# An attention and feed-forward kernel: one scale for each unit of the first weight, sums of weight blocks moved, products of a block scheme reordered, elu written with a rectifier

## The chip, the cores and the metric

The kernel runs on one core of a Trainium2 chip. The metric is the device time in microseconds (us) of one execution. The engines are named as in the profile: TensorE (PE, its weight loads PEld), VectorE (DVE), ScalarE (ACT), GpSimd (POOL) and SyncE (SP), which issues nearly all DMA transfers. Each engine works off its own instructions in order.

## The reference, cut to what matters

```python
# q, k, v: (8, 12, 448, 64) float32; w_in: (768, 2048), w_out: (2048, 768), both float64
scores = q @ k^T / sqrt(64) - log(448)
attn   = sigmoid(scores) @ v
x      = attn.transpose(0, 2, 1, 3).reshape(3584, 768)
h      = x @ w_in
g      = where(h > 0, h, exp(min(h, 0)) - 1)        # elu
out    = g @ w_out                                  # (3584, 768) float32
```

## The kernel before, in words

All products run on TensorE in float16. Each operand is held as two float16 parts: the value times a power of two, rounded (high part, ScalarE), and what is left of it (low part, VectorE). A product is three: high·high, high·low, low·high. The scales are powers of two taken from sums of magnitudes: a matmul with ones (or one with a diagonal, L188, whose result is `pb`) gives them to all partitions, and VectorE takes the exponent.

**Attention.** Twelve heads are six head pairs `hp` per batch. A pair's queries and keys are loaded (`raw`), measured (`measure_next`: maxima on VectorE), scaled (`scale_next`) and split (`split_next`: high parts L606, low parts L609, a transposing DMA L614 from `nat` to `qk`, the split values, and then `load_pair`, which issues the eight loads of a later pair on SP's queue). The main loop (from L1481) runs over batches 2 to 7 and their pairs: scores (L643), sigmoid (ScalarE L667), split of the sigmoid (L687, L688), products with the values (L701). Between these, `fill` puts in matmuls of the second layer of the batch before (L1102).

**First layer.** `w_in` is prepared in the first stage in eight units of 256 columns. Its tokens stand in a hand-written string, `ORDER`, run from left to right; the order on each engine is the order in the program. Per unit: `l` load, `A` `b` `B` `d` bit operations that make float32 of float64, `C` the sum of magnitudes on TensorE, `D` the scale on VectorE, `E` the high part on ScalarE (L323), `F` the low part on VectorE. `C` of two units writes one PSUM tile, and `D`, after the second `C`, makes one scale for both (`swi`, L308); so `E` of the first unit waits for the second unit. Batches 0 and 1 use these parts directly, in the first stage. In the same string `X0` to `X95` are second-layer steps of batch 0, `K` is one step of the sums told next, `W` a store of plain weight blocks.

**Block scheme.** From batch 2 on the first layer is done with seven products of blocks instead of eight (the scheme of Strassen and Winograd), for each of four column groups `w` of two units. The weight enters as seven blocks: three plain ones and four sums and differences. They lie in a DRAM tensor, `blend`, and 168 loads of 384 KB (a ring of ten) bring them back to the space of `wi`. The plain ones are stored by DMA straight from `wi` (`store_parts`). The sums are made once, by the generator `sums_of_parts` (L344): per unit VectorE adds high and low part (L357) and forms the sums; then each of the four is split again, high part on ScalarE (L363), low part on VectorE (L366), into one of three rooms of the tile `room`, which SP's queue stores (L373). A room is used again by the piece three further on, whose high part waits until that store has landed. `make_sums(n)` does n steps, of which a unit has eight: 29 tokens `K` beside the second layer of batch 0, sixteen calls beside the first layer of batch 1 (`beside_first`), and the rest in batch 2's attention, five per pair in pairs 0 to 2 and what remains in pair 3, after which the ring's first ten loads are issued.

The products of a batch run in the order `USES` (L936), each of 18 matmuls (L993) into a PSUM bank: products 1, 4, 6 and 7 into X (which `w` shares), 2 into A, 3 into B, 5 into Y. `behind(k, w)` is what follows product k on the other engines: copies that hand a partial sum on (X to A, L1063 X to B, Y to `s5`), adds of `s5` (L1042, into `c`), and elu. Elu is three operations:

```python
nc.scalar.activation(e, src, AF.Exp, scale=m)                                  # L1007
nc.vector.tensor_scalar(e, e, 1.0, -1.0, op0=ALU.min, op1=ALU.add)             # L1011
nc.vector.scalar_tensor_tensor(e, src, m, e, op0=ALU.mult, op1=ALU.max)        # L1012
```

Half of a column group is done as one tile of 896 columns (`e2`), the other as two of 448 (`e1`). `parts_of_g` splits the result into `g` (L1026, L1031). `order_of_blocks` says after which of the 28 products a part of the next pairs' preparation is put in.

## Time and profile before

| | |
|---|---|
| runs | 1209.97, 1215.53, 1210.32 us; median 1210.32 |
| profiled execution | 1208.79 us, span 1207.0 us |
| mean granted TensorE clock | 0.986 |
| TensorE busy | 1128.0 us, 93% of the span (weight loads 719.1, beside it) |
| VectorE busy | 865.7 us, 72% |
| ScalarE busy | 706.8 us, 59% |
| GpSimd busy | 65.3 us, 5% |
| DMA | 164.65 MB, mean 136 GB/s |

The span is the part of the profiled execution between its first and last instruction. Busy times of different engines overlap; a share is a mean over stages. The stages stand in the trace, from the span's start, at: the preparation of `w_in` and the attention of batches 0 and 1 up to 125 us, first and second layer of batch 0 to 247, first layer of batch 1 to 309, then for each of batches 2 to 7 attention (beside the second layer of the batch before) and block stage: 309 to 414.6 and 414.6 to 470.2 for batch 2.

### The profile page before, as it was taken

What the parts mean: (1) busy time and instruction counts of PE and PEld (TensorE: products, weight loads), DVE (VectorE), ACT (ScalarE), POOL (GpSimd) and SP (SyncE); (2) the same over time, 40 slices, a digit from 0 to 9 for tenths busy, and PEclk for the clock granted to TensorE, in tenths of its full rate; (3) what the DMA queues carried; (4) which work ended last, traced back from release to release, by engine and by line L of the source; (5) the groups of instructions that cost most, each with busy time, mean ns of one, the idle gap of its engine ahead of it and who ended that gap; (6) DMA issues with size and microseconds to landing.
All of it is one profiled execution on the core that took longest, in us unless ns stands there. A gap on an engine that the chain in (4) does not pass through costs nothing.

```text
span 1207.0 us, 22288 instructions
## 1 busy us (share of the span) xinstructions
PE 1128.0 (93%) x8626; PEld 719.1 (60%) x8626; DVE 865.7 (72%) x1783; ACT 706.8 (59%) x996; POOL 65.3 (5%) x276
## 2 busy tenths in 40 slices
PE   6788998889889999999899999999899999999998
PEld 2332454445445597559855697559855597559965
DVE  2777788777878577887777577887777577877600
ACT  5778765434656446684666556685566556685500
POOL 0000000100001000100001000100001000100000
PEclk9899999989999999999999999999999999999999
DMA  9883533444146376445834177445835167425200
GB/s 237 204 233 91 183 108 112 157 149 96 40 109 178 103 227 210 97 91 179 246 93 98 48 212 226 97 90 154 261 94 103 52 200 237 97 45 169 75 27 27
DMA packets 234714, 164.65 MB, mean 136 GB/s; under 512 B 170096, under 2 KB 209008, under 8 KB 234608
## 3 DMA queue, kind: packets, MB, share of 16 engines
q1 hardware_dynamic: 234608, 163.23, 49.1%
q8 instruction: 67, 1.10, 0.4%
q14 instruction: 39, 0.32, 0.1%
HBM read 124.65 MB, written 22.02 MB: 122 GB/s over the span
## 4 chain that ended last, share of the span: by engine, by line
PE 58%; DVE 20%; ACT 9%; DMA 6%; issue 4%; SPq 2%; POOL 1%; DVEq 0%; ACTq 0%; POOLq 0%
PE po L1102 22%; PE psc L643 7%; PE pav L701 6%; PE X L993 6%; PE po_r L1102 5%; PE ph L894 4%; DVE g L1031 2%; PE A L993 2%; PE Y L993 2%; ACT sg L667 2%; DMA vn<-in_v_dram 1%; PE pav L719 1%; DVE ea L1012 1%; PE B L993 1%; DVE nat L609 1%
## 5 line engine op out<-in xcount | busy, mean ns | idle before, releaser
L1102 PE MATMUL po<-wo,g 128*128 128x384 f16 x2304 | 391.6, 328 | 7.0 <-DVE wo L466 4.5
L1102 PEld LDWEIGHTS <-g 128*128 128x128 f16 x2688 | 258.9, 98 | 211.0 <-issue 46.7
L993 PEld LDWEIGHTS <-wi 128*128 128x128 f16 x3024 | 288.6, 98 | 25.1 <-issue 23.7
L688 DVE SCALAR_TENSOR_TENSOR at<-sg,at 128x896 f16<-128x896 f32 x126 | 132.5, 1087 | 62.3 <-ACT at L687 62.0
L993 PE MATMUL X<-wi 128*128 128x224 f16 x1296 | 133.0, 259 | 9.1 <-DVE c L1042 6.6
L667 ACT ACTIVATE sg<-psc,bias,sc 128x896 f32<-128x896 f32 x108 | 114.3, 1090 | 35.6 <-PE psc L643 35.4
L643 PE MATMUL psc<-qk 64*128 64x448 f16 (+2 forms) x960 | 109.8, 379 | 8.3 <-ACT qk L1286 3.7
L606 ACT ACTIVATE nat<-raw,sc 128x384 f16<-128x384 f32 (+1 forms) x108 | 52.8, 536 | 109.7 <-POOL sc L577 103.6
L894 PE MATMUL ph<-xh,wi 128*128 128x448 f16 x576 | 114.0, 359 | 0.0
L687 ACT ACTIVATE at<-sg 128x896 f16<-128x896 f32 x126 | 113.4, 945 | 0.6
L894 PEld LDWEIGHTS <-wi 128*128 128x128 f16 x576 | 56.8, 99 | 59.2 <-issue 9.0
L609 DVE SCALAR_TENSOR_TENSOR nat<-raw,sc,nat 128x384 f16<-128x384 f32 (+1 forms) x108 | 52.5, 526 | 28.3 <-ACT nat L606 27.7
L701 PE MATMUL pav<-at,vn 128*64 128x448 f16 x648 | 69.0, 358 | 0.0
L1102 PE MATMUL po_r<-wo,g 128*128 128x384 f16 x384 | 67.1, 335 | 0.0
L1007 ACT ACTIVATE eb<-c,msc 128x896 f32<-128x896 f32 x24 | 25.0, 1042 | 66.5 <-DVE c L1042 66.5
L643 PEld LDWEIGHTS <-qk 64*128 64x128 f16 (+1 forms) x864 | 30.3, 97 | 52.9 <-issue 32.7
L1112 DVE TENSOR_SCALAR o<-po,osc 128x384 f32<-128x384 f32 x48 | 29.3, 611 | 41.6 <-PE po L1102 38.6
L993 PE MATMUL X<-xh,wi 128*128 128x224 f16 x432 | 45.4, 259 | 9.6 <-DVE ea L1012 9.6
L701 PEld LDWEIGHTS <-vn 128*64 128x64 f16 x648 | 33.9, 110 | 33.0 <-issue 14.2
L1031 DVE SCALAR_TENSOR_TENSOR g<-ea,msc,g 128x448 f16<-128x448 f32 x48 | 32.5, 678 | 17.8 <-ACT g L1026 17.8
L993 PE MATMUL Y<-xh,wi 128*128 128x224 f16 x432 | 45.3, 259 | 0.0
L993 PE MATMUL A<-xh,wi 128*128 128x224 f16 x432 | 45.3, 259 | 0.0
(166 smaller groups left out, 1409.3 us busy)
## 6 DMA issues: line engine op xcount, KB each, us to landing
wi<-blend SPq DMA_DIRECT2D x168, 384.0 KB, 4.6
stage<-in_moe_w_in_dram SPq DMA_DIRECT2D x16, 768.0 KB, 7.1
wo<-in_moe_w_out_dram SPq DMA_DIRECT2D x13, 768.0 KB, 4.5
raw<-in_q_dram SPq DMA_DIRECT2D x96, 96.0 KB, 3.3
raw<-in_k_dram SPq DMA_DIRECT2D x96, 96.0 KB, 2.9
out_dram<-o SPq DMA_DIRECT2D x48, 192.0 KB, 1.9
rv<-in_v_dram SPq DMA_DIRECT2D x36, 192.0 KB, 2.7
blend<-room SPq DMA_DIRECT2D x32, 192.0 KB, 1.9
```

The lines of the kernel that those rows point to most:

```text
L606: nc.scalar.mul(hi, src, s)
L609: nc.vector.scalar_tensor_tensor(lo, src, s, hi, op0=ALU.mult, op1=ALU.subtract)
L643: nc.tensor.matmul(psc[:, j, :S] if g < NC else psc[rows[x], j, :S], kk[rows[j], o], qq[rows[j], :S], start=(n == 0), stop=(n == n_parts - 1),
L667: a = nc.scalar.activation(sg, psc[:, :, :S], AF.Sigmoid, bias=bias, scale=scale)
L687: nc.scalar.mul(parts[0], sg, 2.0**ATOP)
L688: nc.vector.scalar_tensor_tensor(parts[1], sg, 2.0**ATOP, parts[0], op0=ALU.mult, op1=ALU.subtract)
L701: nc.tensor.matmul(pav[rows[j], :S], vv[i][:, j * NC + g if g < NC else 2 * NC + j], sg[k][:, j], start=(g == 0 and n == 0), stop=False,)
L894: nc.tensor.matmul(ph[:, :S], wi[:, NU - 1 - f // WF, f % WF * NK + c, wj], hidden_of(b, c)[:, xj], start=(n == 0), stop=(n == 3 * NK - 1),)
L993: nc.tensor.matmul(to[:, j * HS : (j + 1) * HS], block[:, j, c, wj], rhs(k, c, xj), start=(k in (1, 5) and j == 0 and n == 0), stop=(j == ...
L1031: nc.vector.scalar_tensor_tensor(rows_of_g(w, 1, odd, lo, hi), x, gs, rows_of_g(w, 0, odd, lo, hi), op0=ALU.mult, op1=ALU.subtract,)
L1102: nc.tensor.matmul(po[:, :HM], lh(gj, f), wo[:, i, f, wj], start=(n == 0), stop=(n == 3 * NF - 1),)
L1112: nc.vector.tensor_scalar(o, po[:, :HM], sc, None, op0=ALU.mult)
```

## The change

- Each weight unit gets its own scale (`D` after each `C`); that of a pair's second unit is at least that of its first. Where two units are used together, from batch 2 on, the second unit's scale `wq` holds, and `wt`, the ratio of a unit's own scale to it, is multiplied into sums and plain blocks. `wi` is laid out with rows of 256 columns and one load per unit.
- Plain blocks are no longer stored from `wi`: ScalarE copies their two parts, scaled, into the three rooms (two instructions each). A unit now has seven steps, each with one or no store. 19 tokens `K` are left beside the second layer, none after `X86`; beside batch 1's first layer a step stands only at the eleven turns without other work.
- In batch 2's attention the steps stand behind `scale_next` (two) and behind `split_next` and `measure_next` (three; in pair 3 all the rest, then the ring's loads). `measure_next` of pair 0 is called earlier.
- The products of the block stage are reordered, with the places of the copies, of the splits and of the preparation.
- Elu in the block stage: exp and rectifier on ScalarE, the second in place in PSUM (or `c`), then one instruction on VectorE, min(e - 1, relu). All of `e1` is split at once.

```diff
-V1.1 C0 b1 l2 V1.2 v12 V1.3 A1 M1 v4 T2 v5 H1 n1 H0 T3 I1 Y2 Q1 q5 I0 Y3 S2.0 S2.1 G2.0
-N1 G2.1 S2.2 B1 V2.0 G2.2 q4 S3.3 d0 b2 S3.0 V2.1 G3.3 M2 l3 V2.2 C1 S3.1 k5 D1 G3.0 E0
...
-X50 K h10 X51 p10 X52 h11 X53 p11 X54 h12 X55 p12 X56 h13 X57 h14 p13 p14 X58 K h15 X59
-h16 p15 p16 X60 h17 X61 h18 p17 p18 X62 K W0 X63 X64 K O3 X65 K X66 W1 X67 K X68 K X69
-X70 K W2 X71 K X72 X73 K X74 K W3 X75 X76 K X77 K X78 W4 X79 K X80 K O4 X81 X82 K W5 X83
-K X84 X85 K X86 K W6 X87 X88 K X89 K X90 W7 X91 K X92 K X93 X94 K X95 K O5
+V1.1 C0 b1 l2 V1.2 D0 v12 V1.3 A1 M1 v4 T2 v5 H1 n1 H0 T3 I1 Y2 Q1 q5 I0 Y3 S2.0 S2.1
+G2.0 N1 G2.1 S2.2 B1 V2.0 G2.2 q4 S3.3 d0 b2 S3.0 V2.1 G3.3 M2 l3 V2.2 E0 S3.1 k5 C1
...
+X58 K h15 X59 h16 p15 p16 X60 h17 X61 h18 p17 p18 X62 K X63 X64 K O3 X65 X66 K X67 X68 K
+X69 X70 K X71 X72 K X73 X74 K X75 X76 K X77 X78 K X79 X80 K O4 X81 X82 K X83 X84 K X85
+X86 K X87 X88 X89 X90 X91 X92 X93 X94 X95 O5
...
+            queue.dma_start(st.bitcast(U64), src[:, :, u * WF * P : (u + 1) * WF * P])
...
         def scale():
+            least = [wp[:, f.start - 1 : f.start]] if u % 2 else []
+            sum_magnitude(wp[:, f], st["sums"][:, : WF * P], *least)
...
+        nc.gpsimd.tensor_tensor(wt, wp, wr, op=ALU.mult)
...
     def sums_of_parts():
...
+        def high(x):
+            t = next_out()
+            nc.scalar.mul(t[1][:, 0], block(full, x), r)
+            return t
+
+        def low(x, t):
+            nc.vector.scalar_tensor_tensor(
+                t[1][:, 1], block(full, x), r, t[1][:, 0], op0=ALU.mult, op1=ALU.subtract
+            )
+            store(t, {"22": 3, "21": 1, "11": 0, "12": 2}[x])
...
+        def copy(x, slot):
+            t = next_out()
+            for h in range(2):
+                nc.scalar.mul(t[1][:, h], block(wi[:, NU - 1 - u, h], x), r)
+            store(t, slot)
 
         for u in range(NU):
+            r = wt[:, u * WF : u * WF + 1]
+            parts = wi[:, NU - 1 - u]
+            for i in range(2):
+                c = slice(i * HK, (i + 1) * HK)
+                nc.vector.tensor_tensor(full[:, c], parts[:, 0, c], parts[:, 1, c], op=ALU.add)
+                copy("11" if i else "12", 4 + (not i))
+                yield
             add("22", "21", "22", ALU.add)
             add("21", "11", "21", ALU.subtract)
+            copy("22", 6)
             yield
             add("11", "22", "11", ALU.subtract)
             add("12", "12", "11", ALU.subtract)
+            one = high("22")
             yield
+            two = high("21")
+            low("22", one)
             yield
+            one = high("11")
+            low("21", two)
             yield
+            two = high("12")
+            low("11", one)
             yield
+            low("12", two)
...
     USES = [(1, 0), (5, 0)]
-    for w in range(NW):
...
-        USES += [(6, w), (2, w), *ahead[0], (7, w), (3, w), *ahead[1], (4, w)]
+    for w in range(NW - 1):
+        late = [(6, w + 1), (4, w)] if w == NW - 2 else [(4, w), (6, w + 1)]
+        USES += [(6, 0)] * (not w) + [(2, w), (5, w + 1), (7, w), (1, w + 1), (3, w), *late]
+    USES += [(k, NW - 1) for k in (2, 7, 3, 4)]
...
         def exps(e, src, w):
-            a = nc.scalar.activation(e, src, AF.Exp, scale=m[:, 0, 4 * w : 4 * w + 1])
+            scale = m[:, 0, 4 * w : 4 * w + 1]
+            nc.scalar.activation(e, src, AF.Exp, scale=scale)
+            a = nc.scalar.activation(src, src, AF.Relu, scale=scale)
...
-        def rests(e, src, w):
-            nc.vector.tensor_scalar(e, e, 1.0, -1.0, op0=ALU.min, op1=ALU.add)
-            nc.vector.scalar_tensor_tensor(
-                e, src, m[:, 0, 4 * w : 4 * w + 1], e, op0=ALU.mult, op1=ALU.max
-            )
+        def rests(e, src):
+            nc.vector.scalar_tensor_tensor(e, e, -1.0, src, op0=ALU.add, op1=ALU.min)
...
     def beside_first(f):
-        for step in order.get(f, []):
+        for step in order.get(f, [make_sums]):
             step()
-        make_sums()
...
                 for t in range(2):
                     p.halves(t)
-                if b == 2 and hp <= HK:
-                    make_sums()
+                if hp == 0:
+                    measure_next()
...
                 p.scores(2)
                 p.sigmoid(2)
-                if hp == 0:
-                    measure_next()
...
                 p.halves(2)
                 if hp % 2:
                     first.halves(NC)
-                if b == 2 and hp <= HK:
-                    make_sums()
...
                     scale_next()
                     pb_tag = "pav1"
+                    if b == 2:
+                        make_sums(2)
...
                     done[1].finish()
-                if b == 2 and hp <= HK:
-                    make_sums()
-                if b == 2 and hp == HK:
-                    make_sums(8 * NF)
-                    for i in range(RING):
-                        load_block(i)
...
                     split_next()
-                    if b == 2 and hp < HK:
-                        make_sums(2)
                     measure_next()
+                    if b == 2:
+                        make_sums(3 if hp < HK else 8 * NF)
+                    if b == 2 and hp == HK:
+                        for i in range(RING):
+                            load_block(i)
```

## Rows read from the trace of the kernel before

**Rows 1.** Busy time by stretch: start:end, length, busy us per engine, granted clock, DMA.

```profile
0.00:125.00 125.00, 97.94 (x511) 37.05 (x511) 80.49 (x160) 92.12 (x91) 1.81 (x15) 0.96 0.76 188
...
247.00:309.00 62.00, 57.49 (x292) 28.87 (x290) 47.56 (x115) 27.37 (x59) 4.68 (x15) 0.94 0.34 97
309.00:414.60 105.60, 94.29 (x663) 49.13 (x661) 78.31 (x163) 61.91 (x86) 7.80 (x26) 0.94 0.42 117
414.60:470.20 55.60, 51.92 (x528) 50.03 (x524) 41.31 (x90) 28.41 (x47) 3.70 (x17) 1.00 0.69 204
...
1088.80:1139.90 51.10, 51.10 (x526) 49.95 (x523) 35.06 (x68) 25.89 (x42) 0.61 (x2) 1.00 0.47 144
```

The columns are PE, PEld, DVE, ACT and POOL, each with its count of instructions, then the granted clock, the DMA share and GB/s.

**Rows 2.** Waits: engine and line, waited for, us in total, times, longest us.

```profile
ACT wi L323 <- DVE swi L308: 8.4, 4, 3.0
...
PE pav L701 <- ACT sg L667: 6.5, 3, 2.5
...
PE psc L643 <- ACT qk L1286: 3.7, 2, 3.5
```

**Rows 3.** TensorE in time, 240 to 420: start, us, instruction, idle before it.

```profile
255.08 0.17 PE L188 MATMUL pb<-dg,ones 128*128 128x4 bf16 x1 [4.51 <-DVE dg L182]
...
317.75 0.74 PE L643 MATMUL psc<-qk 64*128 64x448 f16 x6 [1.51 <-ACT sg L667]
...
325.05 0.17 PE L188 MATMUL pb<-dg,ones 128*128 128x12 bf16 x1 [3.04 <-DVE dg L182]
...
357.95 0.17 PE L188 MATMUL pb<-dg,ones 128*128 128x12 bf16 x1 [4.39 <-DVE room L366]
...
397.20 2.12 PE L643 MATMUL psc<-qk 64*128 64x448 f16 x12 [2.27 <-DMA qk<-nat]
```

**Rows 4.** All engines in order of time, 344 to 360.

```profile
347.13 1.55 SPq L614 DMA_TRANSPOSE qk<-nat  x1
...
349.30 0.74 PE L643 MATMUL psc<-qk 64*128 64x448 f16 x6
...
351.39 0.23 DVE L182 TENSOR_SCALAR dg<-blocks,trm 128x12 bf16<-128x12 bf16 x1
...
354.50 3.80 SPq L373 DMA_DIRECT2D blend<-room  x4
356.85 0.51 ACT L363 CAST room<-room 128x384 f16<-128x384 f32 x1 [5.76 <-DMA blend<-room]
...
357.80 1.09 ACT L667 ACTIVATE sg<-psc,bias,sc 128x896 f32<-128x896 f32 x1
```

**Rows 5.** The tile `room` from 200 to 420: instructions, ns min/median/max.

```profile
L357 DVE TENSOR_TENSOR room<-room x32: 540/558/559, 208.3 to 369.6; 128x384 f32<-128x384 f32 x32
L363 ACT CAST room<-room x32: 494/510/513, 213.9 to 378.1; 128x384 f16<-128x384 f32 x32
...
DMA to landing us min/median/max: 1.8/1.9/4.4
```

**Rows 6.** TensorE in time, 414.6 to 470.4: its waits in batch 2's block stage.

```profile
437.50 1.89 PE L993 MATMUL X<-xh,wi 128*128 128x224 f16 x18 [0.83 <-DVE ea L1012]
...
450.83 1.89 PE L993 MATMUL X<-xh,wi 128*128 128x224 f16 x18 [1.09 <-DVE ea L1012]
...
463.56 1.89 PE L993 MATMUL X<-wi 128*128 128x224 f16 x18 [0.49 <-ACT B L1063]
...
468.45 1.89 PE L993 MATMUL X<-wi 128*128 128x224 f16 x18 [1.27 <-DVE c L1042]
```

**Rows 7.** Groups by line and form: busy us, mean ns; idle before, releasers.

```profile
L1007 ACT ACTIVATE eb<-c,msc 128x896 f32<-128x896 f32 x24 | 25.0, 1042 | 66.5 <-DVE c L1042 66.5
L1011 DVE TENSOR_SCALAR ea<-ea 128x448 f32<-128x448 f32 x48 | 18.6, 388 | 5.4 <-ACT ea L1007 5.4
...
L1007 ACT ACTIVATE ea<-A,msc 128x448 f32<-128x448 f32 x24 | 15.0, 624 | 23.8 <-DVE msc L876 23.4
...
L1061 ACT ACT_TABLE_LOAD x6 | 7.7, 1283 | 0.1
```

More of the change, by code (lines that the diff above doesn't have):

```diff
@@ L250, in signed, with sum_magnitude @@
         )
-    def sum_magnitude(dst, sums):
+    def sum_magnitude(dst, sums, *least):
         m = sb.tile([P, 1], F32, tag="alw", name="alw", bufs=2)
         nc.vector.tensor_reduce(m, sums, axis=AX.X, op=ALU.max)
-        nc.vector.tensor_scalar(m, m, TINY, None, op0=ALU.max)
+        more = {"op1": ALU.max} if least else {}
+        nc.vector.tensor_scalar(m, m, TINY, *(least or [None]), op0=ALU.max, **more)
         nc.vector.tensor_scalar(
@@ L291, in sums @@
         def sums():
[L292 to L308 removed]
+            st["sums"] = ps.tile([P, 512], F32, tag="pm", name=f"si{u}", bufs=PB)
+            add_sums(st["sums"][:, : WF * P], st["t"], True, True, ones_in)
+        def scale():
+            least = [wp[:, f.start - 1 : f.start]] if u % 2 else []
+            sum_magnitude(wp[:, f], st["sums"][:, : WF * P], *least)
+            s = st["s"] = sb.tile([P, 1], F32, tag="sw", name=f"swi{u}", bufs=2)
+            nc.vector.reciprocal(s, wp[:, f][:, 0:1])
         def lower():
             nc.vector.scalar_tensor_tensor(
[L312 removed]
+                d[:, 1], st["t"], st["s"], d[:, 0], op0=ALU.mult, op1=ALU.subtract
             )
@@ L343, in sums_of_parts @@
+        nc.gpsimd.tensor_tensor(wt, wp, wr, op=ALU.mult)
     def sums_of_parts():
-        names = "11", "12", "21", "22"
         n = HK * P
         room = sb.tile([P, 7, 2 * n], F16, tag="xh", name="room")
-        one = {x: room[:, i].bitcast(F32) for i, x in enumerate(names)}
-        slots = {"22": 3, "21": 1, "11": 0, "12": 2}
-        def whole_of(u, i):
-            x = room[:, 2 * i : 2 * i + 2].bitcast(F32).rearrange("p b (c x) -> p (b c) x", x=P)
-            hi, lo = (wi[:, NU - 1 - u, i * NK : (i + 1) * NK, h] for h in range(2))
-            nc.vector.tensor_tensor(x, hi, lo, op=ALU.add)
@@ L356, in add @@
-        def add(x, y, z, op):
-            nc.vector.tensor_tensor(one[x], one[y], one[z], op=op)
-        def parts(i):
-            return room[:, 4 + i % 3].rearrange("p (c h x) -> p h c x", c=HK, h=2)
-        def high(x, i):
-            nc.scalar.copy(parts(i)[:, 0], one[x].rearrange("p (c x) -> p c x", c=HK))
-        def low(x, i):
-            nc.vector.tensor_tensor(
-                parts(i)[:, 1], one[x].rearrange("p (c x) -> p c x", c=HK), parts(i)[:, 0],
-                op=ALU.subtract,
-            )
@@ L371, in store, with block, next_out @@
-        def store(u, x, i):
+        full = room[:, :4].rearrange("p b x -> p (b x)").bitcast(F32)
+        full = full.rearrange("p (c x) -> p c x", c=NK)
+        def block(t, x):
+            c, f = HK * (x[1] == "2"), P * (x[0] == "2")
+            return t[:, c : c + HK, f : f + P]
+        def add(x, y, z, op):
+            nc.vector.tensor_tensor(block(full, x), block(full, y), block(full, z), op=op)
+        out = 0
+        def next_out():
+            nonlocal out
+            out += 1
+            t = room[:, 4 + out % 3]
+            return t, t.rearrange("p (c h x) -> p h c x", c=HK, h=2)
@@ L372, in store @@
+        def high(x):
[5 more added lines that the diff above has]
+                t[1][:, 1], block(full, x), r, t[1][:, 0], op0=ALU.mult, op1=ALU.subtract
+            )
+            store(t, {"22": 3, "21": 1, "11": 0, "12": 2}[x])
+        def store(t, slot):
             w, j = divmod(u, 2)
[L373 to L375 removed]
```

216 lines of the change are left out of this document (87 added, 129 removed).

## The prediction, made before the changed kernel had run

> **What bounds the kernel now.** I read four views in this order. First the table of busy time by stretch. Of the six block stages (the first layer of batches 2 to 7) the first is 55.6 us long with 3.7 us of TensorE idle, the next four are within 0.3 us of it, and the sixth, 51.1 us, has no idle time [rows 1]. So from 414.6 us on there is little more to win than those 3.7 us a batch, while whatever delays TensorE is paid in full. The other idle time stands before 414.6 us: 27 us in the first 125, 4.5 in 247 to 309, 11.3 in 309 to 414.6, and there the granted clock is below 1 as well. A mean of 0.94 means 12% of the stretch at the lower level: 7.4 us of 62.0 and 12.7 us of 105.6, of which half is lost, 3.7 and 6.3 us [rows 1]. Then the waits and TensorE's own gaps, which say what ended the idle time: in the first stage ScalarE, which had itself waited four times (8.4 us) for the weight scale of step D [rows 2]; later the sums of the weight blocks [rows 3, 4]; in the block stage the results that free a PSUM bank [rows 6].
>
> **The change part by part.** The sum is made against the profiled execution, 1208.8 us (span 1207.0). The median of the runs shown is 1210.3, so 1.5 us are added at the end.
>
> *First stage (0 to 125 us).* The scale was taken for two weight units together, so E of the first unit had to wait for C and D of the second. Now each unit has its own D, placed ahead of its E. ScalarE's four waits go [rows 2], and with them most of TensorE's waits behind them, 6.5 us in three for a sigmoid and 3.7 in two for a copy of queries and keys [rows 2]. Against that, four more D stand in VectorE's queue; I allow 1 us for each. The weight load is one transfer a unit with rows twice as long, whose gain I put at nothing. ScalarE is 74% busy there [rows 1] and takes back part of what it wins. Bounds: 10 us won (all four), 4 us lost (the added D on the path). I take 5 won.
>
> *Second layer of batch 0 and start of batch 1 (to 255 us).* Of 29 steps of sums beside the second layer 19 remain, and none stands after its product 86. VectorE's queue ends earlier, and the measure that the clearing matmul at 255.08 waited 4.51 us for comes in time. A step now has one store behind it and pieces in three rooms; a piece passes in about 0.51 + 0.56 + 1.9 = 3.0 us (copy, low part, store) [rows 5], so three rooms allow a step in 1.0 us. From product 64 on there are twelve steps, where the old order had 22 and came 4.5 us late. I take the 4.5 us and the 3.7 us of low clock behind them, 8 won; bounds 8 won, none.
>
> *Attention of batch 2 (309 to 414.6 us).* This is the term that decides. Steps done when batch 2 begins: 19 beside the second layer and 11 beside batch 1's first layer (five of its sixteen turns have other work). There are 7 a unit, 57 with the tail. In head pairs 0 to 3, two steps stand behind the scale and three (in pair 3 all that are left) behind the split of the next pair. The split issues a transpose and then eight loads on SP's queue. The trace has what that does to a store behind them: transpose issued at 347.13, store at 354.50, and ScalarE, which needed that room, goes on at 356.85, 9.7 us after the transpose [rows 4]. Now the queue behind the waiting ScalarE instruction is worse: in the old order the stopped copy stood behind the next pair's sigmoids, in the new one it stands ahead of them. TensorE reaches the pair's third scores 2.2 us after the transpose [rows 4] and needs the PSUM buffer that the first sigmoid frees. Counting the steps, a high part whose low part and store come one step later is the second of the two in pairs 0, 2 and 3 (steps 32, 42, 47), so its store falls behind the loads, and the piece three further on stops ScalarE.
> - Pair 0 to 1: 9.7 + 0.5 (high part) + 1.1 (sigmoid) - 2.2 = 9.1 us of TensorE waiting.
> - Pair 1 to 2: no store is late (step 37 is a plain copy), but the high part waits for four adds of 0.56 us behind the measure, which ends 4.5 us after the transpose [rows 4, 5], about 1.0 less without the two low parts ahead of it: 3.5 + 2.2 + 1.0 + 1.1 - 2.2 = 5.6 us.
> - Pair 2 to 3: the stopped piece is a copy of two parts, 9.7 + 1.0 + 1.1 - 2.2 = 9.6 us.
> - Pair 3 to 4: nine pieces remain. The third stops until 9.7 us; three copies of two parts follow (to 12.7), then four high parts, each after the store three pieces back has landed: the first three at 12.7, 13.6 and 14.6, the fourth, behind the first one's low part and store, at 15.7, to 16.2. 16.2 + 1.1 - 2.2 = 15.1 us.
>
> Together 39 us. TensorE comes later to each of these than in the old run, since the clock falls behind long waits, as it did behind those of 4.39 and 4.51 us [rows 1, 3], and that eats part of the next wait. So I take 34 and add nothing for the clock. What goes: the waits of 1.51, 4.39 and 2.27 us [rows 3] (the last because the ring's ten loads now stand behind the transpose) and 4.6 of the 6.3 us of low clock, 12.8 in all; the wait of 3.04 us for pair 0's measure stays with its share of the clock, because on VectorE the measure still stands behind two low parts of the attention, though it is called earlier. Net 21 lost. Bounds: all 39 and 6 of clock less 8.2, 37 lost; no new wait, 12.8 won.
>
> *Block stages.* Each loses four waits, 0.83, 1.09, 0.49 and 1.27 us [rows 6], if nothing is late after them. The reordering puts four products instead of two between the last use of bank X and its reuse, and two instead of one behind the copy of B, so the first three go, 2.4 us. The last one grows. The rectifier moves work to ScalarE: 4 x (2 x 0.62 + 1.04) = 9.1 us a batch on top of 28.4 busy, while VectorE loses at least 4 x 3 x 0.39 = 4.7 [rows 1, 7]. Taking VectorE's pieces as long as ScalarE's of the same size, behind the product (4,2) come exp and rectifier (to 1.2), VectorE's minimum (1.9), the high part that waits for it (2.9), exp and rectifier (4.2) and a high part (5.2); then on VectorE a low part (6.3) and the add that frees X (6.9). The product (4,3) is due three products later, at 5.4, by the two that take 3.6 us between the last two of [rows 6]. That is 1.5 us, and about 1 more because exp and rectifier over 896 columns stand ahead: 2.5 instead of 1.27. One measure now stands close to its scale, 0.5 to 0.9 us by my estimate of its place. Net nothing in five batches (bounds 3.7 won and 3 lost in each); the sixth, which had no wait, loses 2.
>
> The rectifier could need another table on ScalarE. The table loads here cost 1.28 us each and there are six for each of the two changes a batch [rows 7], where one of the two lines stands; no rectifier runs in this trace, so no row says whether it changes tables. The Trainium skill (ScalarE: Activation LUTs, "Table sets: the hidden batching unit") says that cheap functions such as relu are in every set. By that rule no load is added and the sum stays; without it there is the fourth rival below.
>
> *The rest.* Ratios, joint scales and the two scales in the moe constants are a few VectorE and GpSimd instructions of under 0.5 us beside other work: nothing; at most 1 us if they stood on the path. The low parts as a scaled subtraction cost VectorE some 0.06 us more each, 32 times, behind TensorE: 2 us at most if uncovered.
>
> Sum: -5 - 8 + 21 + 0 + 2 = +10, so 1218.8, and with the 1.5 us of the median 1220.
>
> **The rivals.**
> 1. *The stores are not in the way, and the change is faster.* Place: ScalarE at the piece three steps behind the late store, in pairs 0, 2 and 3. It decides at whether ScalarE comes there later than 9.7 us after the transpose. For it: in the old trace one such store stopped ScalarE once in these pairs, and most steps passed. Against it: the order puts these pieces directly behind the split, with nothing long between. Then the batch-2 term is -13, the block stages give back 1.5 each: 1208.8 - 5 - 8 - 13 - 7 + 2 + 1.5 = 1179, up to 1195 with small waits.
> 2. *Half of it.* The waits come but are about half as long, as TensorE arrives late: 17 instead of 34, 1203, or 1200 to 1212 with the smaller gains ahead of it.
> 3. *ScalarE bounds the block stage.* The wait of 2.5 us draws the clock down, which costs about 1.7 us in each batch (behind the four waits before 414.6 us it was 6.3), and the waits are 1.6 us longer: 6 x 3.3 = 20 on top, 1240. For it: 9 us more on ScalarE and in-order waits on VectorE; against it: waits of 1.27 us left the clock at 1.00 there [rows 1, 6].
> 4. *Table changes.* 12 rectifiers a batch, two loads each: 6 x 24 x 1.28 = 185 us, 1400.
>
> **How the numbers follow.** Forecast 0.50 (its own range 1212 to 1238), rival 1 0.20, rival 2 0.19, rival 3 0.10, rival 4 0.01. Half a per cent, 6 us, is about what a measurement of this kernel can tell from no change. Slower: 0.49 + 0.02 of rival 2 + 0.10 + 0.01 = 0.62; same: 0.01 + 0.14 of rival 2 = 0.15; faster: 0.20 + 0.03 = 0.23. The range 1190 to 1240 leaves out most of rival 1 and half of rival 3.
>
> **What would show it.** In the trace of the changed kernel ScalarE should have long waits for the stores of sums in pairs 0, 2 and 3 of batch 2, and TensorE gaps of 5 to 16 us before the third scores of pairs 1 to 4, ended by a sigmoid; ScalarE's waits for the weight scale and the 4.51 us gap should be gone; in the block stages only the wait before the last product should be left, near 2.5 us. No such ScalarE waits would make the prediction wrong towards faster; block stages clearly under 53 us would too, and ones over 58 us towards slower.

## The result and the profile after

| | before | after |
|---|---|---|
| median of nine runs | 1209.84 us | 1218.48 us |
| profiled execution (span) | 1208.79 (1207.0) | 1217.69 (1215.9) |
| mean granted clock | 0.986 | 0.981 |
| TensorE busy | 1128.0 | 1124.6 |
| VectorE, ScalarE busy | 865.7, 706.8 | 833.0, 774.7 |

The ratio is 1.0085, with a 95% interval of 1.0063 to 1.0108: slower, by 9 to 10 us. The nine runs of the changed kernel lie in two groups, five at 1217.4 to 1218.5 us (the profiled one among them) and four at 1222.2 to 1223.0, so the ratio, which counts all of them, is above that of the medians, 1.0071. TensorE did no more work than before; it stood idle longer, 91.3 us of the span against 79.0, and most of what was added stands in one place. The table shows the stages as the traces have them (first and last matmul of each):

| stage | before | after | difference | forecast |
|---|---|---|---|---|
| up to batch 0's first layer | 127.0 | 113.8 | -13.2 | -5 |
| batch 0's two layers | 120.0 | 120.8 | +0.8 | } -8 |
| batch 1's first layer | 62.3 | 54.8 | -7.5 | } |
| attention of batch 2 | 105.3 | 131.7 | +26.4 | +21 |
| block stages, batches 2 to 6 | 55.6 to 55.9 | 54.1 to 54.2 | -7.9 in all | 0 |
| block stage, batch 7 | 51.3 | 53.0 | +1.7 | +2 |
| attentions, batches 3 to 7 | 72.8, 88.5 | 74.0, 89.8, one 91.5 | +7.9 in all | not in the sum |
| last layer | 66.9 | 67.5 | +0.6 | 0 |

The busy time by stretch of the changed kernel, in the columns of [rows 1]: up to batch 0's first layer, batch 1's first layer, attention and block stage of batch 2, the attentions of batches 3 and 6, and the last block stage.

```profile
0.00:113.80 113.80, 96.36 (x524) 36.68 (x524) 83.81 (x185) 92.70 (x91) 2.04 (x16) 1.00 0.77 210
...
234.60:289.30 54.70, 54.70 (x295) 28.12 (x292) 44.23 (x111) 30.77 (x65) 4.75 (x15) 1.00 0.29 79
289.30:421.00 131.70, 95.16 (x662) 49.13 (x661) 85.26 (x169) 75.65 (x110) 10.10 (x26) 0.87 0.41 119
421.00:475.30 54.30, 51.88 (x530) 50.12 (x528) 35.54 (x76) 34.39 (x54) 3.65 (x17) 1.00 0.78 219
475.30:549.30 74.00, 72.06 (x565) 37.44 (x564) 59.68 (x124) 56.98 (x73) 5.73 (x26) 1.00 0.40 100
875.60:967.10 91.50, 89.36 (x662) 47.38 (x662) 62.56 (x128) 57.40 (x74) 5.73 (x26) 0.98 0.34 85
1095.40:1148.40 53.00, 51.50 (x528) 50.12 (x525) 28.88 (x54) 31.16 (x49) 0.61 (x2) 1.00 0.44 139
```

Read the third line first: TensorE is busy 95.2 us there (94.3 before), but idle 36.5 (11 before). The second line has no idle time at all and the full clock, where [rows 1] had 4.5 us idle and 0.94. TensorE in order of time shows where the 36.5 us stand:

```profile
301.82 0.17 PE L190 MATMUL pb<-dg,ones 128*128 128x12 bf16 x1 [1.34 <-DVE dg L184]
...
319.62 2.57 PE L639 MATMUL psc<-qk 64*128 64x448 f16 x18 [9.67 <-ACT sg L663]
...
339.68 1.19 PE L639 MATMUL psc<-qk 64*128 64x448 f16 x6 [4.04 <-ACT sg L663]
...
362.72 2.57 PE L639 MATMUL psc<-qk 64*128 64x448 f16 x18 [7.72 <-ACT sg L663]
...
393.63 1.30 PE L639 MATMUL psc<-qk 64*128 64x448 f16 x6 [13.78 <-ACT sg L663]
```

Four gaps before the third scores of pairs 1 to 4, all ended by a sigmoid: 35.2 us, against 9.1, 5.6, 9.6 and 15.1 worked out and 34 taken. The gaps of 1.51, 4.39 and 2.27 us in [rows 3] are gone, and so is the one of 4.51 us ahead of them. The first line is the wait for pair 0's measure, 1.34 us where it was 3.04. What holds the sigmoid up is in the next rows, all engines at the change from pair 0 to 1:

```profile
307.96 1.10 ACT L356 ACTIVATE room<-room,wt 128x384 f16<-128x384 f32 x2
...
308.12 1.57 SPq L610 DMA_TRANSPOSE qk<-nat  x1
...
311.48 0.23 DVE L184 TENSOR_SCALAR dg<-blocks,trm 128x12 bf16<-128x12 bf16 x1
...
311.62 1.67 DVE L360 SCALAR_TENSOR_TENSOR room<-room,wt 128x384 f16<-128x384 f32 x3
...
314.84 0.62 SPq L520 DMA_DIRECT2D rv<-in_v_dram  x1
315.56 1.50 SPq L367 DMA_DIRECT2D blend<-room  x3
317.97 0.61 ACT L356 ACTIVATE room<-room,wt 128x384 f16<-128x384 f32 x1 [8.90 <-DMA blend<-room]
318.49 2.07 ACT L663 ACTIVATE sg<-psc,bias,sc 128x896 f32<-128x896 f32 x2
```

Two high parts, then ScalarE waits 8.9 us for a room. The low parts that fill the rooms come behind the next pair's maxima (`dg` is their last step), at 311.62; the stores stand behind the loads on SP's queue, the last of which is issued at 314.84. The store lands 9.85 us after the transpose was issued (9.7 in [rows 4]), and the sigmoids stand behind the piece it frees.

### The profile page after: what moved, and what is told of

Read it like the earlier page. It is cut to its first block, busy times and chain, and to the rows that moved or that the text cites. A ratio compares the mean times of both kernels' runs of the same rounds, so it can differ in the third digit from the quotient of the medians.

```text
span 1215.9 us, 22314 instructions
## 1 busy us (share of the span) xinstructions
PE 1124.6 (92%) x8626; PEld 718.4 (59%) x8626; DVE 833.0 (69%) x1705; ACT 774.7 (64%) x1092; POOL 67.1 (6%) x277
## 4 chain that ended last, share of the span: by engine, by line
PE 46%; ACT 12%; DVE 9%; issue 3%; DMA 1%; SPq 1%; POOL 0%; ACTq 0%; DVEq 0%; POOLq 0%
PE po L1098 21%; PE X L988 6%; PE psc L639 5%; PE pav L697 5%; PE po_r L1098 4%; ACT g L1015 2%; PE Y L988 2%; DVE c L1036 1%; ACT eb L999 1%; ACT c L1000 1%; PE A L988 1%; ACT ea L999 1%; DVE mt L212 1%; ACT sg L663 1%; PE pav L715 1%
## 5 line engine op out<-in xcount | busy, mean ns | idle before, releaser
L1098 PE MATMUL po<-wo,g 128*128 128x384 f16 x2304 | 395.8, 330 | 6.8 <-DVE wo L462 3.8
L602 ACT ACTIVATE nat<-raw,sc 128x384 f16<-128x384 f32 (+1 forms) x108 | 52.3, 536 | 101.4 <-POOL sc L573 88.5
L890 PE MATMUL ph<-xh,wi 128*128 128x448 f16 x576 | 111.0, 352 | 0.0
L890 PEld LDWEIGHTS <-wi 128*128 128x128 f16 x576 | 55.9, 98 | 52.5 <-issue 0.7
L1004 DVE SCALAR_TENSOR_TENSOR eb<-eb,c 128x896 f32<-128x896 f32 x24 | 26.2, 1092 | 60.8 <-ACT c L1000 60.8
L578 POOL TENSOR_SCALAR sc<-pw 128x1 f32<-128x1 f32 x36 | 9.6, 267 | 669.6 <-DVE pw L196 669.6
L988 PE MATMUL B<-xh,wi 128*128 128x224 f16 x432 | 45.3, 259 | 0.0
```

Of the source, the lines that this page charges most:

```text
L602: nc.scalar.mul(hi, src, s)
L890: nc.tensor.matmul(ph[:, :S], wi[:, NU - 1 - f // WF, wj, c, f % WF * P :][:, :P], hidden_of(b, c)[:, xj], start=(n == 0), stop=(n == 3 * ...
L988: nc.tensor.matmul(to[:, j * HS : (j + 1) * HS], block[:, j, c, wj], rhs(k, c, xj), start=(k in (1, 5) and j == 0 and n == 0), stop=(j == ...
L1004: nc.vector.scalar_tensor_tensor(e, e, -1.0, src, op0=ALU.add, op1=ALU.min)
L1098: nc.tensor.matmul(po[:, :HM], lh(gj, f), wo[:, i, f, wj], start=(n == 0), stop=(n == 3 * NF - 1),)
```

## The experiments

The first four change only where things stand in batch 2's attention. Each ratio is to the kernel before, timed beside it.

**The loads behind the sums.** In batch 2's pairs 0 to 3 `load_pair` is called after the sums:

```diff
-        load_pair(at + 2)
+        held.append(at + 2)
+        if not hold:
+            load_pair(held.pop())
...
+    hold, held = False, []
...
+                    hold = b == 2 and hp <= HK
                     split_next()
                     measure_next()
                     if b == 2:
                         make_sums(3 if hp < HK else 8 * NF)
+                    hold = False
+                    while held:
+                        load_pair(held.pop())
```

> The changed kernel with one edit: in pairs 0 to 3 of batch 2 the eight loads that the split issues for a later pair stand behind the steps of sums on SP's queue, no longer ahead of their stores. The changed kernel's four gaps before the third scores of batch 2 are 9.67, 4.04, 7.72 and 13.78 us, 35.2 together. My theory: the store that ScalarE waits for stands behind these loads, but also, by less, behind the next pair's maxima on VectorE: its low part begins 3.5 us after the transpose (311.62 against 308.12), so with the loads gone the store lands some 3.4 us earlier (314.5 instead of 317.9). Three gaps get 3.4 us shorter, 4.04 stays: about 25 in all, 1207 us. Rival, loads alone: nothing else stands in the way, the store goes out right behind the transpose, each of the three gets 6 us shorter: 17 in all, 1199 us. Rival, work: it is the added pieces on ScalarE and VectorE themselves, in whatever order: 35 us stay, 1218 us.

Measured: 1209.5 us, ratio 1.0007 (0.9989 to 1.0024). The gaps, TensorE in order of time:

```profile
317.80 2.57 PE L639 MATMUL psc<-qk 64*128 64x448 f16 x18 [5.95 <-ACT sg L663]
...
337.86 0.74 PE L639 MATMUL psc<-qk 64*128 64x448 f16 x6 [3.54 <-ACT sg L663]
...
357.14 2.57 PE L639 MATMUL psc<-qk 64*128 64x448 f16 x18 [3.92 <-ACT sg L663]
...
384.15 1.30 PE L639 MATMUL psc<-qk 64*128 64x448 f16 x6 [9.21 <-ACT sg L663]
```

22.6 us: the three long ones are 3.7, 3.8 and 4.6 shorter, as the low part's place behind the maxima allows, not 6. So the loads, taken out alone, are worth about a third of the gaps. The rival that only the work counts falls. The kernel is 2.5 us above the forecast all the same; in this trace the first stage, whose code is that of the changed kernel, ends at 115.8 us and not at 113.8.

**The sums ahead of the maxima**, the loads left where they are:

```diff
                     split_next()
-                    measure_next()
                     if b == 2:
                         make_sums(3 if hp < HK else 8 * NF)
+                    measure_next()
```

> The changed kernel with one edit: in batch 2 the steps of sums behind the split stand ahead of the next pair's maxima on VectorE, as before the change, and no longer behind them; the eight loads stay ahead of the stores on SP's queue. My theory: the store is still behind the loads, so the three long gaps stay within 0.7 us; only the gap of 4.04 us, which comes from four adds behind the maxima, falls to under 1. Sum of the four gaps about 31, 1214 to 1215 us. Rival, maxima: the low parts behind the maxima are what is late, each gap falls by about 3.4 us: 22 in all, 1205. Rival, work: 35 stay, 1218.

Measured: 1218.6 us, ratio 1.0082 (1.0056 to 1.0108). The gaps:

```profile
320.31 2.57 PE L639 MATMUL psc<-qk 64*128 64x448 f16 x18 [9.57 <-ACT sg L663]
...
337.52 0.74 PE L639 MATMUL psc<-qk 64*128 64x448 f16 x6 [1.16 <-ACT sg L663]
...
361.34 2.57 PE L639 MATMUL psc<-qk 64*128 64x448 f16 x18 [10.13 <-ACT sg L663]
...
392.07 1.30 PE L639 MATMUL psc<-qk 64*128 64x448 f16 x6 [14.23 <-ACT sg L663]
```

The second fell as expected, 4.04 to 1.16, yet the sum stayed at 35.1 where I had 31. The third grew by 2.4. Behind the shorter gap the clock did not fall (granted 1.00 from there to the third, 0.89 in the changed kernel), so the matmuls between the two took 13.7 us instead of 15.3, and TensorE stood at the third scores 2.1 us after the transpose instead of 4.2. The store was no earlier: ScalarE goes on 10.1 us after the transpose, 9.8 in the changed kernel. Time won ahead of a late store is waited for at it. By the sum alone the rival "work" would stand; that single gaps move with single places speaks against it.

**Both**, sums ahead of the maxima and of the loads, with `load_pair` changed as in the first:

```diff
+                    hold = b == 2 and hp <= HK
                     split_next()
-                    measure_next()
                     if b == 2:
                         make_sums(3 if hp < HK else 8 * NF)
+                    hold = False
+                    while held:
+                        load_pair(held.pop())
+                    measure_next()
```

> Both edits: in batch 2 the sums ahead of the maxima on VectorE and ahead of the eight loads on SP's queue. My theory: the low part comes right behind the split, its store right behind the transpose, landing about 3.6 us after it; with the high part and one sigmoid TensorE waits 3.4 instead of 9.67, under 1 instead of 4.04, 1.5 instead of 7.72 and some 8 instead of 13.78 (nine pieces remain there in three rooms, 1 us each): 14 in all, 1196 us, less what the maxima, now late, cost at the next scale (up to 4 us in pair 3). Rival, work: 35 stay, 1218.

Measured: 1201.2 us, ratio 0.9945 (0.9929 to 0.9962). Three gaps are left, of 4.34, 4.28 and 9.12 us; the one of 4.04 is gone. They make 17.7 us where I had 14, most of the miss in the second (1.5 expected), and the kernel is 5 us above the forecast. All engines at the change from pair 0 to 1:

```profile
309.57 1.57 SPq L610 DMA_TRANSPOSE qk<-nat  x1
...
310.21 1.67 DVE L360 SCALAR_TENSOR_TENSOR room<-room,wt 128x384 f16<-128x384 f32 x3
311.24 1.99 SPq L367 DMA_DIRECT2D blend<-room  x3
...
314.08 0.61 ACT L356 ACTIVATE room<-room,wt 128x384 f16<-128x384 f32 x1 [3.56 <-DVE mx L565]
...
315.73 1.82 PE L639 MATMUL psc<-qk 64*128 64x448 f16 x10 [4.34 <-ACT sg L663]
```

The store goes out 1.7 us after the transpose and ScalarE goes on 4.5 us after it. That row names the maxima as what ended ScalarE's wait, which this instruction does not read; it comes 2.8 us after the store's issue, so I read it as that store's landing. Together the two places cost 17 us. Taken out alone, the loads are worth 9 and the maxima nothing: the late loads hide all that the maxima cost, and the late maxima hide half of what the loads cost.

**The old places** of the sums in batch 2, all else as changed:

```diff
                 for t in range(2):
                     p.halves(t)
+                if b == 2 and hp <= HK:
+                    make_sums()
...
                 if hp % 2:
                     first.halves(NC)
+                if b == 2 and hp <= HK:
+                    make_sums()
...
-                    if b == 2:
-                        make_sums(2)
...
+                if b == 2 and hp <= HK:
+                    make_sums()
+                if b == 2 and hp == HK:
+                    make_sums(8 * NF)
+                    for i in range(RING):
+                        load_block(i)
...
                     split_next()
+                    if b == 2 and hp < HK:
+                        make_sums(2)
                     measure_next()
-                    if b == 2:
-                        make_sums(3 if hp < HK else 8 * NF)
-                    if b == 2 and hp == HK:
-                        for i in range(RING):
-                            load_block(i)
```

> The changed kernel with the steps of sums of batch 2's attention at the places of the kernel before (one behind the first two splits of the sigmoid, one behind the third, one behind the scale, two behind the split and ahead of the maxima; in pair 3 all that are left ahead of its split, then the ring's loads). The steps themselves (scaled copies on ScalarE, seven a unit) are the changed kernel's. My theory: the places make the loss, so the attention of batch 2 falls from 131.7 us to 106 to 110 (it was 105.3 before the change; 27 steps are left at its start instead of 19) and the kernel to 1193 to 1197 us, below the kernel before. Rival, work: the copies and the larger number of steps cost ScalarE the time wherever they stand: attention of batch 2 over 120 us, kernel over 1207.

Measured: 1203.3 us, ratio 0.9960 (0.9946 to 0.9974); the attention of batch 2 takes 115.6 us, where I had 106 to 110. The places account for 16 of the 26 us. What is left I put down to the number of steps, 27 at the start of this attention and 19 before the change (argued, not tried at these places; the last run below tries fewer steps at the new ones). The longest ScalarE wait for a room is now 6.96 us, and TensorE's longest gap, in pair 3, is 7.69:

```profile
375.55 1.30 PE L639 MATMUL psc<-qk 64*128 64x448 f16 x6 [7.69 <-ACT sg L663]
```

**One more step at each turn.** The kernel of both edits, and beside batch 1's first layer `make_sums()` at all sixteen turns: 22 steps remain.

```diff
-        for step in order.get(f, [make_sums]):
+        for step in order.get(f, []):
             step()
+        make_sums()
```

> The kernel of both edits (sums ahead of the maxima and of the loads, 1201.2 us) with one more: beside batch 1's first layer a step of sums stands at all sixteen turns, as before the change, not at the eleven without other work, so batch 2's attention begins with 22 steps left instead of 27; only pair 3 has fewer (7, not 12). My theory: the gap before pair 4, 9.12 us there, is the pieces' own time, about 1 us each in three rooms, and five steps fewer make it 4 to 5 us; the first layer of batch 1 (54.7 us) stays within 1 us: kernel 1195 to 1197. Rival, paid back: the five steps make the measures of batch 2's first pairs late, the first layer of batch 1 gets 3 us or more longer and the gap is only moved: 1200 or more.

Measured: 1198.7 us, ratio 0.9918 (0.9890 to 0.9947). Its interval overlaps that of the kernel of both edits, so the 2.5 us between the two medians are not clear of noise; the traces show what changed. Batch 1's first layer is as fast as before (54.7 us in both), batch 2's attention falls from 114.9 to 109.4, its last gap from 9.12 to 4.07, 1 us for each of the five steps, as expected. But the sum of the gaps hardly fell, as two lines show, first of the kernel of both edits:

```profile
290.80:405.70 114.90, 95.83 (x662) 49.26 (x661) 84.84 (x169) 75.65 (x110) 10.07 (x26) 0.90 0.47 137
```

and of this one:

```profile
290.10:399.50 109.40, 91.09 (x662) 48.32 (x660) 83.19 (x169) 73.32 (x106) 10.45 (x26) 0.97 0.46 137
```

Idle time is 19.1 and 18.3 us, busy time 95.8 and 91.1 for the same matmuls: of the 5.5 us, 4.7 are the clock, whose mean is 0.97 with gaps of up to 4.8 us, where it was 0.90 with one of 9.12. Arriving sooner, TensorE waits a little more at other places (2.56 and 4.77 us at the worst). That the whole is 2 us above the forecast comes from elsewhere: the five later attentions take 408.4 us in this trace, 403.3 in that of both edits, since the clock fell in four of the five, where it fell in one there, at 1.7 us each (the last section has more on this).

**The first stage: two loads a unit, and the late scales.** The first of two edits, each on the changed kernel alone, gives `load_w_in` two transfers of 128 columns:

```diff
-            queue.dma_start(st.bitcast(U64), src[:, :, u * WF * P : (u + 1) * WF * P])
+            words_of = st.bitcast(U64)
+            for i in range(WF):
+                f = (u * WF + i) * P
+                queue.dma_start(words_of[:, :, i * P : (i + 1) * P], src[:, :, f : f + P])
```

> The changed kernel with each weight unit loaded by two transfers of 128 columns, as before the change, in the place of one of 256. TensorE reaches the first layer of batch 0 at 113.8 us in the changed kernel and at 127.0 in the kernel before; I had forecast 5 us for that and it was 13.2. My theory: the separate scale did it (E no longer waits for the second unit), the loads give nothing: first layer from 113 to 116 us, kernel within 3 us of the changed one, 1217 to 1221. Rival, loads: the longer rows brought the weights earlier, and that is the unexplained 8 us: first layer from 120 to 124 us, kernel 1225 to 1228.

The second takes the old order of the first stage's tokens, with `D0` directly ahead of `D1`, and so on, and `E` behind both:

```diff
...
-V1.1 C0 b1 l2 V1.2 D0 v12 V1.3 A1 M1 v4 T2 v5 H1 n1 H0 T3 I1 Y2 Q1 q5 I0 Y3 S2.0 S2.1
-G2.0 N1 G2.1 S2.2 B1 V2.0 G2.2 q4 S3.3 d0 b2 S3.0 V2.1 G3.3 M2 l3 V2.2 E0 S3.1 k5 C1
+V1.1 C0 b1 l2 V1.2 v12 V1.3 A1 M1 v4 T2 v5 H1 n1 H0 T3 I1 Y2 Q1 q5 I0 Y3 S2.0 S2.1 G2.0
+N1 G2.1 S2.2 B1 V2.0 G2.2 q4 S3.3 d0 b2 S3.0 V2.1 G3.3 M2 l3 V2.2 C1 S3.1 k5 D0 D1 G3.0
+E0 Q2 k4 G3.1 S3.2 N2 F0 V3.0 A2 V3.1 R0 G3.2 B2 b3 V3.2 V3.3 T4 H2 d1 H3 T5 q6 Y4 C2 v7
...
```

> The changed kernel with the first stage's order of before: each unit keeps its own scale, but D of the first unit stands directly ahead of D of the second, and E behind both, so E waits for the second unit again. My theory: the first layer of batch 0 starts at 125 to 128 us again (113.8 in the changed kernel, 127.0 before), kernel 1229 to 1233. Rival, loads: it stays at 118 or earlier, kernel under 1224.

Measured: with two loads 1224.0 us, ratio 1.0125 (1.0096 to 1.0155); with late scales 1228.8, ratio 1.0173 (1.0146 to 1.0199). The first matmul of batch 0's first layer, two loads:

```profile
117.66 12.66 PE L893 MATMUL ph<-xh,wi 128*128 128x448 f16 x66
```

and late scales:

```profile
122.63 7.55 PE L890 MATMUL ph<-xh,wi 128*128 128x448 f16 x39
```

3.9 and 8.8 us later than 113.8, 12.7 together, of 13.2. In the nine traces of kernels with the changed kernel's first stage this matmul starts between 113.6 and 115.8 us, so the 8.8 are well clear of that spread, and of the 3.9 only some 2 are; the interval with two loads overlaps that of the changed kernel. Neither text had it right: the loads are worth something, though less than the rival needs, and the scales alone don't bring 127.0 back. With two loads ScalarE waits 5.0 us for the transfers, 2.3 in the changed kernel and 3.7 in the run with the loads behind the sums. The Trainium skill (DMA: Bandwidth & Descriptors, "Bandwidth") gives the rule to put at least 1 MiB in a transfer to have 75% of peak or more, from transfers that GpSimd issues; 768 KB against 1536 KB, issued by SP, agrees in direction, with 2 to 4 us for eight units. Row length and the number of issues on SP change with the size here, and no run takes them apart.

**The old elu** in the block stage, in the new order of products:

```diff
-            a = nc.scalar.activation(src, src, AF.Relu, scale=scale)
...
-            nc.vector.scalar_tensor_tensor(e, e, -1.0, src, op0=ALU.add, op1=ALU.min)
+            nc.vector.tensor_scalar(e, e, 1.0, -1.0, op0=ALU.min, op1=ALU.add)
+            nc.vector.scalar_tensor_tensor(
+                e, src, m[:, 0, 4 * w : 4 * w + 1], e, op0=ALU.mult, op1=ALU.max
+            )
```

> The changed kernel with elu in the block stage as before the change (exp on ScalarE, then two instructions on VectorE, no rectifier); the order of products and of the splits is the new one. In the changed kernel the block stages of batches 2 to 6 take 54.2 us (55.7 before), and the attentions behind them 74.0 and 89.8 or more (72.8 and 88.5), because the first maxima's matmul waits 2.0 instead of 0.7 us. My theory: the order of products gives the 1.5 us, and the rectifier on ScalarE makes the attention late: block stages 54 to 55, attentions 72.8 to 73.3, kernel 1211 to 1214. Rival, rectifier: it is VectorE's relief that made the block stage shorter: block stages 55.5 or more, attentions 74 as in the changed kernel, kernel 1224 or more. Rival, split: it is the larger last split (896 columns at once) that makes the attention late, the rectifier is neutral in both: 54.2, 74.0, kernel 1218.

Measured: 1215.6 us, ratio 1.0067 (1.0042 to 1.0093), an interval that overlaps the changed kernel's; the stages tell more. The attentions are 72.9 and 88.7 us again, as before the change: the rectifier makes them late. The block stages stay at 54.6 in even batches, so the order of products, with the changes of places that came with it, gives most of the 1.5 us there; in odd batches they take 55.9 and 55.3, and little of it is left. TensorE at the start of the attention behind batch 2, in the kernel before:

```profile
482.17 0.17 PE L188 MATMUL pb<-dg,ones 128*128 128x12 bf16 x1 [0.72 <-DVE dg L182]
```

in the changed kernel, with its waits in the block stage ahead of it:

```profile
450.31 0.17 PE L190 MATMUL pb<-dg,ones 128*128 128x12 bf16 x1 [0.36 <-DVE dg L184]
...
450.83 3.61 PE L988 MATMUL X<-wi 128*128 128x224 f16 x36 [0.36 <-DVE c L1036]
...
473.40 1.88 PE L988 MATMUL X<-wi 128*128 128x224 f16 x18 [1.70 <-DVE c L1036]
...
488.34 0.17 PE L190 MATMUL pb<-dg,ones 128*128 128x12 bf16 x1 [1.95 <-DVE dg L184]
```

and with the old elu:

```profile
474.28 1.88 PE L988 MATMUL X<-wi 128*128 128x224 f16 x18 [2.00 <-DVE c L1038]
...
488.07 0.17 PE L190 MATMUL pb<-dg,ones 128*128 128x12 bf16 x1 [0.80 <-DVE dg L184]
```

The wait for the maxima, 1.95 us, goes to 0.80; the wait before the last product goes from 1.70 to 2.00. Behind the odd batch of 55.9 us, where that wait is 2.26, its 18 matmuls take 2.79 instead of 1.88: the clock fell.

**The old elu in the last column group only**, on the kernel of the run with one more step at each turn:

```diff
-            nc.scalar.activation(e, src, AF.Exp, scale=scale)
-            a = nc.scalar.activation(src, src, AF.Relu, scale=scale)
+            a = nc.scalar.activation(e, src, AF.Exp, scale=scale)
+            if w < NW - 1:
+                a = nc.scalar.activation(src, src, AF.Relu, scale=scale)
...
+            if w < NW - 1:
+                nc.vector.scalar_tensor_tensor(e, e, -1.0, src, op0=ALU.add, op1=ALU.min)
+                return
+            nc.vector.tensor_scalar(e, e, 1.0, -1.0, op0=ALU.min, op1=ALU.add)
...
```

> The kernel with the sums ahead of maxima and loads and a step at all sixteen turns of batch 1's first layer (1198.7 us), and elu without the rectifier (exp on ScalarE, two instructions on VectorE) in the last of the four column groups of each block stage only; the first three keep the rectifier. With the old elu everywhere the attentions fell to 72.9 and 88.7 us but the block stages of odd batches grew to 55.9 and 55.3. My theory: only the last group delays the attention behind it, and only the first three gain in the block stage; so attentions 72.8 to 73.3 and 88.5 to 89 with the full clock, block stages 54.1 to 54.6, kernel 1189 to 1193 us. Rival: the wait before the last product, 1.70 us with the rectifier and 2.00 without, grows further with the groups before it on ScalarE, block stages 55.5 and more: 1196 or more.

Measured: 1190.7 us (1189.8 to 1191.3), ratio 0.9844 (0.9826 to 0.9862). The attentions take 72.9 and 88.7 us, all five, the block stages of batches 2 to 6 54.4 to 55.1. Attention of batch 2, its block stage and the attention of batch 3, by stretch:

```profile
289.90:399.40 109.50, 91.19 (x662) 48.41 (x661) 83.26 (x169) 73.47 (x106) 10.47 (x26) 0.97 0.45 136
399.40:453.90 54.50, 51.88 (x530) 50.11 (x528) 36.15 (x78) 33.62 (x52) 3.68 (x17) 1.00 0.79 220
453.90:526.80 72.90, 72.10 (x566) 37.45 (x567) 60.60 (x126) 55.87 (x71) 5.76 (x26) 1.00 0.39 100
```

**The steps beside the second layer as before** (29 tokens `K`, up to that layer's end), on the changed kernel:

```diff
...
-X86 K X87 X88 X89 X90 X91 X92 X93 X94 X95 O5
+X85 K X86 K X87 X88 K X89 K X90 X91 K X92 K X93 X94 K X95 K O5
```

> The changed kernel with the 29 steps of sums beside the second layer of batch 0 where the kernel before has them, up to the end of that layer, in the place of 19 that end at its product 86. My theory: VectorE's queue is then late again for the first measure of batch 1's first layer, so this layer takes 60 to 63 us (54.8 in the changed kernel, 62.3 before) with a gap of 3.5 us or more and a low clock behind it; 17 steps instead of 27 are left for batch 2's attention, whose last gap (13.78 us) falls by 7 or more. Kernel 1212 to 1217 us. Rival: the earlier call and the shorter steps make the layer fast, wherever the steps stand: layer under 57 us, kernel 1206 to 1210.

Measured: 1214.4 us, ratio 1.0039 (1.0023 to 1.0055). Batch 1's first layer takes 64.2 us, 1.2 more than I had at most, and its first measure is late again:

```profile
247.03 0.16 PE L190 MATMUL pb<-dg,ones 128*128 128x4 bf16 x1 [7.93 <-DVE dg L184]
```

Batch 2's attention falls to 113.3 us, since 17 steps remain: at the same four places the gaps are 9.52, 7.88, 1.90 us and none. The first is as long as ever, the second longer (4.04 in the changed kernel), since the other number of steps puts another piece there, for whose room ScalarE waits 8.95 us, and the last, of 13.78, is gone with the pieces that pair 3 no longer has. So the steps taken out of the end of that layer are what made batch 1's first layer fast, and the price of it was paid in batch 2. It also shows that places and number are not two terms of a sum: the old places win 16 us with 27 steps left, ten steps fewer win 18 at the new places, and the loss is 26.

## Why the prediction was right, and where it was not

The forecast was 1220, the measured median 1218.5. The deciding step was right in place and size, and in mechanism but for one cause left out: 35.2 us of gaps against 34 taken, at the four places named, each through the piece named. The step from 39 worked out to 34 held too: TensorE stood at the third scores 1.8 and 2.3 us after the transpose at the first two changes of pair, and 4.2 at the last two, where the 39 has 2.2 for all. That the whole came within 1.5 us is luck: three other terms were off by 8 us each, two of them for the better, and the attention of batch 2 by 5 for the worse, and these nearly cancel.

- **First stage, -5, measured -13.2**, outside its bounds of 10 and -4. Taken back alone, the separate scales were worth 8.8 and the longer loads 3.9, of which 2 lie within the spread of this stage; I had put the loads at nothing without a row for it. ScalarE's waits for a scale went from 8.4 us to none; two of TensorE's, 6.5 and 3.7, became 0.7 and 0.2. I had credited half of what the waits showed, because of the added `D`, and these cost nothing that can be seen.
- **Second layer and batch 1's first layer, -8, measured -6.7.** The wait of 4.51 us and the low clock behind it went, for the reason given (the run with the steps beside the second layer as before brings both back).
- **Attention of batch 2, +21, measured +26.4.** The gaps agree. The 4.6 us of low clock that I counted as won did not come: TensorE's busy time there is 95.2 us, 94.3 before. Where the old gaps went, the clock now fell behind the new ones (0.87 in that stretch), and I had set that down as nothing. The reason I gave for the stores was too simple as well: I took the loads ahead of them as the cause, and the low parts behind the maxima are nearly as late. Taking out the loads wins 9 us, the maxima 0, both together 17. Beyond the gaps the clock costs some 4 us there (busy 91.1 at 0.97 in the run with one more step at each turn). The wait for pair 0's measure, which was to stay at 3.04 us, fell to 1.34.
- **Block stages, 0, measured -7.9.** Of the four waits in [rows 6] the first three went, as said. The last was to grow to 2.5 and is 1.70, a measure's is 0.36 instead of 0.5 to 0.9, and a wait of 0.36 us before a product remains. The sum of them is 2.4 instead of 3.7. Last batch +1.7 for +2.
- **Attentions of batches 3 to 7, no term, measured +7.9.** This is what I left out. I followed the rectifier and the last split only to the end of the block stage; the work that they push past its end stands on ScalarE ahead of the next attention's sigmoids, and VectorE's maxima behind those come 1.2 us late (both runs with the old elu take that back). In one of the five the clock fell besides, 1.7 us.
- **Rival 1** (faster, 1179 to 1195) did not come: the stores are in the way. With them and the maxima out of it the kernel is at 1201.2; it comes into that range only with five steps moved and the old elu in the last column group besides (1190.7). **Rival 2** (half of the waits) did not come either: 35.2 us, not 17. **Rival 3** did not come: the waits in the block stage were shorter than I had put them, and the clock stayed at 1.00 there. **Rival 4** is excluded: the changed kernel has the same table loads as before and none for the rectifier. The two groups, by line and form:

```profile
L1054 ACT ACT_TABLE_LOAD x6 | 7.7, 1283 | 0.1
L1079 ACT ACT_TABLE_LOAD x6 | 7.7, 1283 | 0.1
```

The rule of the Trainium skill (ScalarE: Activation LUTs, "Table sets: the hidden batching unit"), that cheap functions lie in every set, agrees with this trace for the set that was loaded for exp: 72 rectifiers ran with no load added.

## What to carry to other kernels

When work is moved behind a step, write down for each engine and queue what then stands between its parts: here the piece on ScalarE, its low part behind maxima on VectorE and its store behind eight loads on SP's queue met in one room, and the in-order engine passed the wait on to TensorE. Two such causes at one wait hide each other, so taking out one tells little; take out both before judging. The number of steps that are left decides which of them stands at such a place, so count them anew after each move. And follow an added instruction past the end of its stage: the engine that ends a stage late begins the next one late.

## What was not expected of the hardware

- Transfers of rows twice as long brought the first layer of batch 0 earlier by 3.9 us over eight units of 1.5 MB (2 to 4 by the spread of this stage), though the DMA share of the first stage was 0.77 with them and 0.79 with the shorter ones.
- Behind waits of the same length at the start of an attention the clock of the changed kernel fell in one place and not in another: it stayed at 1.00 behind 2.13 us in batch 4, and behind 2.14 us in batch 6 thirty matmuls took 6.72 us (5.04 at the full clock). That attention is 1.7 us longer. In the kernels with these waits it came in one to four of the five attentions, in the two with the old elu, where the wait is at most 0.98, in none. What decides between the two stays open. The two places in the changed kernel:

```profile
616.65 0.17 PE L190 MATMUL pb<-dg,ones 128*128 128x12 bf16 x1 [2.13 <-DVE dg L184]
...
888.83 0.17 PE L190 MATMUL pb<-dg,ones 128*128 128x12 bf16 x1 [2.14 <-DVE dg L184]
888.86 6.72 PE L1098 MATMUL po<-wo,g 128*128 128x384 f16 x30
```
